# A contiguous write and a strided read in an exponential, with a new set of planner priorities

## Chip, cores and metric

The kernel runs on one core of a Trainium2 chip. The metric is the device time in microseconds of one execution. Before the change the median of three runs is 550.88 us (548.93 to 553.61).

## What is computed

Three stages follow each other; each takes the output of the one before. Attention is of the Nyström kind with 32 landmarks, on 4 batches, 8 heads, 576 tokens, 64 features. MoE sends each token to one of 8 experts (capacity 576) and applies two layers. MoE2 is one dense pair of layers with a PReLU between.

```python
q_lm = q.reshape(B, H, m, S // m, D).mean(axis=3)
k_lm = k.reshape(B, H, m, S // m, D).mean(axis=3)
A, Bm, C = sm(q, k_lm), sm(q_lm, k_lm), sm(q_lm, k)      # softmax of scaled scores
Z = Bm.transpose(0, 1, 3, 2) / (norm1(Bm) * norminf(Bm) + 1e-06)
for _ in range(6):
    Z = 2 * Z - Z @ Bm @ Z
attn = A @ Z @ C @ v
...
logits = x @ w_gate                                      # x: 2304 x 512
expert_idx = np.argmax(logits, axis=1)
h = np.maximum(np.einsum('ecd,edf->ecf', disp, w1), 0.0)  # 512 -> 1024
y = np.einsum('ecf,efd->ecd', h, w2)                      # 1024 -> 512
out[i] = gate_w[i] * y[expert_idx[i], pos[i]]
...
h = x @ w_in                                              # 512 -> 2048
g = np.maximum(h, 0.0) + alpha * np.minimum(h, 0.0)
return g @ w_out                                          # 2048 -> 512
```

## The kernel before

**Work.** Attention goes by (batch b, group g of four heads), eight pairs. MoE and MoE2 then go by entry: an entry is one pair of a batch and an expert that has tokens there. With these inputs there are three. The first entry is done ahead of a loop, in one stretch with attention; the loop at L1796 does the other two. Products are made from two or three products of 16-bit halves, so weights are scaled by a power of two and split into a high and a low half (`split`, for WI and WO; MW for an expert's first layer, W for its second). The scale of a weight comes from a sum of squares (`squares`), which one small matmul adds up over partitions (`scale_of`: the matmul that reads ss_w1, ss_w2, ss_wi or ss_wo), and a few narrow VectorE operations behind it (tot, sc, s, r).

An entry has four stages on TensorE: the first MoE layer (`moe_h`: mm<-xT,MW), the second (`moe_y`: mm<-W,hgA), the first MoE2 layer (`moe2_h`: mm<-yA,WIa and mm<-yB,WIa, 256 and 320 tokens wide, later WIb), and the second (`moe2_out`: mm<-WO,hgA, then hgB). An expert's first layer uses only 32 landmark rows: 16 matmuls turn W1 into them (`landmark_rows`), and MW is their scaled, split form. The tiles hgA and hgB hold MoE2's hidden values. The weights of the next entry are loaded and converted while an entry runs (`next_w1_late`, `next_w2`); W1 is loaded over tiles that the raw WO occupied. The stores of zeros to the output (`clear`, out<-zero) stand in SP's queue, as all plain loads.

**Order.** Each engine takes its instructions strictly in its queue's order. That order is not written by hand. Operations are yielded by generators, the streams, and `Plan.run` (L346) issues them one at a time from a model of durations. It takes the operation with the earliest modelled start; another stream with a better (lower) rank that uses the same engine goes first if it starts before `by()`. The rank of a stream is a constant in the source, and many are set anew on the way.

```python
def by(self, s, x):
    return s.start + min(s.op.ns, self.patience + self.EAGER * (s.rank - x.rank))
```

`.takes(us)` sets the modelled duration of an operation. `keep_warm` (L248) puts filler matmuls (L1728, mm<-zero,ones or big<-zero,ones, 128x256) into a fresh PSUM tile where the model lets TensorE wait. The loop body is planned anew by the same function with few streams of fixed ranks.

**The exponential of C.** `attend_c` (L672) makes the scores of 32 landmarks against 576 tokens for four heads in a PSUM tile `big` of two banks, takes the maximum (mx) and its scaled negative (nm), and ScalarE writes the exponential to EC in SBUF with its row sum. Four transposes on TensorE read EC, the copy to CT follows, and then the product with v.

Of the kernel before, what the change touches and what calls it, by code (L numbers as in the profile page):

```python
# [18 lines left out]
LM = 32  # L19
TG = 18  # L20
# [4 lines left out]
RANKS = [[-19.821, -51.876], [-35.858, 62.800], [-39.803, -18.825], [-37.270, -58.893]]  # L25
# [179 lines left out]
class Plan:  # L205
# [5 lines left out]
    EAGER = -30.723  # L211
# [173 lines left out]
class Kernel:  # L385
# [41 lines left out]
    def constants(self):  # L427
# [29 lines left out]
        self.streams["constants"].own = -31.506  # L457
# [72 lines left out]
    def loads(self):  # L530

        for b in range(self.B):
            for g in range(2):
                heads = slice(4 * g, 4 * g + 4)
                self.streams["loads"].own = RANKS[b][g] + -31.591
                for nm, src in (("k", self.k), ("q", self.q)):
                    self.raw[nm, b, g] = t = yield Get(self.S["qk"])
                    yield self.dq.dma_start(t, src[b, heads].rearrange("h (p j) d -> (h p) j d", j=TG))
                    self.have.add((nm, b, g))
                if (b, g) == (0, 0):  # L540
                    self.streams["values"] = yield Fork(self.values(), 47.215)

    def values(self):

        for b in range(self.B):
            for g in range(2):
                heads = slice(4 * g, 4 * g + 4)
                if (b, g) != (0, 0):
                    self.streams["values"].own = RANKS[b][g] + -39.752
                self.raw["v", b, g] = t = yield Get(self.S["v"])  # L550
                src = self.v[b, heads]
                yield self.dq.dma_start(t[:, :, :4].rearrange("p h t d -> p h (t d)"), src[:, : 4 * P].rearrange("h (p t) d -> p h (t d)", t=4))
                yield self.dq.dma_start(t[:64, :, 4], src[:, 4 * P :].rearrange("h p d -> p h d"))
                self.have.add(("v", b, g))
                if (b, g) == (0, 0):
                    self.tc.prologue_barrier()

    def sums(self):


        gp = self.gp
        for b in range(self.B):
            for g in range(2):
                self.streams["sums"].own = RANKS[b][g] + -31.456
# [24 lines left out]
    def turn(self):  # L589
# [8 lines left out]
        for b in range(self.B):  # L598
            for g in range(2):
                self.streams["turn"].own = RANKS[b][g] + -19.707  # L600
# [71 lines left out]
    def attend_c(self, b, g):  # L672
# [18 lines left out]
        apart = EC.rearrange("p (m j w) -> p w j m", m=LM, w=2)  # L691
        yield act.activation(apart, tokens.rearrange("p (w j m) -> p w j m", w=2, m=LM), AF.Exp, bias=nm2[:, 0:1], scale=0.125 / TG, accum_out=sums[:, 0:1])
# [41 lines left out]
    def attend_a(self, b, g):  # L734
# [32 lines left out]
        self.streams["store", b, g] = yield Fork(self.store(b, g, parts), 46.670)  # L767
# [8 lines left out]
    def attention_post(self, bs):  # L776
# [79 lines left out]
        if b == 0:  # L856
            self.streams["post0"].own = -44.230
# [53 lines left out]
        for n, bb in enumerate(bs):  # L911
# [18 lines left out]
            if bb == 0:  # L930
                yield from self.first_expert(L[0:1, 0, 0, :])
                self.streams["post0"].own = -38.923
            yield Fork(self.used(bb, AT))
        self.have.add(("x", bs[-1]))
        if b:
            yield self.until(("routed", 0))
            self.streams["post"].own = 12.961
# [37 lines left out]
    def route(self, bs, L):  # L975
# [82 lines left out]
        if b == 0:  # L1058
# [5 lines left out]
            self.streams["post0"].own = 46.684  # L1064
# [138 lines left out]
    def landmark_rows(self, MT, slots, late=0.0):  # L1203
# [26 lines left out]
        scale = yield Fork(self.scale_of("w1", 4), -39.828)  # L1230
# [38 lines left out]
    def early(self):  # L1269
# [12 lines left out]
        self.streams["early_loads"] = yield Fork(loads(), -32.383)  # L1282
# [42 lines left out]
    def convert(self, name, n, amax=None, low="d", load=None, first=0):  # L1325
# [9 lines left out]
        scale = yield Fork(self.scale_of(name, n // 2, amax), -31.812)  # L1335
# [12 lines left out]
    def weight2(self, name, src, amax, low, first=0):  # L1348
# [9 lines left out]
        if name == "wi":  # L1358
            self.streams["wi_loads"] = yield Fork(self.fetch(name, src, range(first, 16, 2), arrived), -58.911)
        else:  # L1360
            self.streams["wo_loads"] = yield Fork(self.fetch(name, src, range(first, 16, 2), arrived), -31.034)
# [246 lines left out]
    def pre(self):  # L1608

        yield self.until(("P", 0, 0), ("P", 0, 1), *([("used", self.n_early - 4)] if self.n_early else ["early"]))  # L1610
        self.streams["first"].own = -38.041
# [4 lines left out]
        self.streams["first"].own = 13.553  # L1616
# [3 lines left out]
        self.streams["first"].own = -20.015  # L1620
# [3 lines left out]
    def weights(self):  # L1624
# [4 lines left out]
        self.streams["rows"] = yield Fork(self.landmark_rows(self.MT[:, 0:2], [self.big] * 2), -30.753)  # L1629
        yield self.until("early")  # L1630
        self.streams["weights"].own = -32.417
        yield from self.load_expert(bass.ds(e0, 1), ["w2"])
        self.streams["weights"].own = 1.715
# [85 lines left out]
    def run(self):  # L1719
# [15 lines left out]
        with tc.manual_schedule(engines={ET.PE, ET.DVE, ET.Activation, ET.Pool, ET.SP}):  # L1735
# [24 lines left out]
            for _ in range(10):  # L1760
# [5 lines left out]
                "constants": Stream(self.constants(), 1.014),  # L1766
                "post0": Stream(self.attention_post([0]), -36.880),
                "first": Stream(self.pre(), -20.351),
                "weights": Stream(self.weights(), -20.511),
                "rooms": Stream(self.rooms(), -33.672),  # L1770
                "post": Stream(self.attention_post(list(range(1, self.B))), -36.946),
                "early": Stream(self.early(), 61.182),
                "wi": Stream(self.weight_in(), -30.891),
                "wo": Stream(self.weight_out(), 52.666),
                "clear": Stream(self.clear(), 17.278),
                "experts": Stream(self.experts(), -66.764),
                "out": Stream(self.first_out(), -40.666),
                "next": Stream(self.first_next(), -44.222),
                "next_w1": Stream(self.next_w1_late(), -44.548),
                "next_w2": Stream(self.next_w2('d'), -68.688),  # L1780
            }
            for b in range(self.B):
                for g in range(2):
                    self.streams["c", b, g] = Stream(self.attend_c(b, g), RANKS[b][g] + -50.062)
                    self.streams["a", b, g] = Stream(self.attend_a(b, g), RANKS[b][g] + 12.563)
# [41 lines left out]
```

## Time and profile before

| | us |
|---|---|
| median of three runs | 550.88 |
| profiled execution | 550.0 |
| its span from first to last instruction | 548.1 |
| TensorE busy | 517.7 (94%) |
| VectorE busy | 297.8 (54%) |
| ScalarE busy | 261.0 (48%) |
| GpSimd busy | 93.6 (17%) |
| mean granted clock of TensorE | 0.992 |

The busy shares are means over stages with different limits, and TensorE's contains the fillers. So the page's shares are read first, then the same shares by stage, and in the stages the timeline: a row of it holds the start, the duration, and in brackets the engine's idle time just before together with what ended it. A row with a count is a run of like instructions; its duration reaches from the first start to the last end, and a matmul's end lies past the start of the next.

### The profile page before, as it was taken

Reading aid. Unit: us, or ns where it says so; the run is one execution under the profiler, and the core shown is the slowest. Engines: PE = TensorE matmul, PEld = TensorE weight load, DVE = VectorE, ACT = ScalarE, POOL = GpSimd, SP = SyncE. Lnnn points to the kernel's source line nnn. Section 1 sums busy time; section 2 is a strip of 40 time slices with the busy share of each in tenths; the row PEclk is TensorE's granted clock in tenths of the full one; section 3 lists DMA queues with packets and bytes.
Section 4 is the critical chain, followed back from the end, with each engine's and each line's share of the span. In section 5 each row is a group of like instructions: output and inputs, shape, how many; then the busy total and the mean of one; then the engine's idle time right before and its main releaser. Section 6 shows DMA issues by size and latency. Waiting matters only on the chain. (4 is left out here: it accounts for less than half of the span.)

```text
span 548.1 us, 12276 instructions
## 1 busy us (share of the span) xinstructions
PE 517.7 (94%) x4888; PEld 341.5 (62%) x4888; DVE 297.8 (54%) x712; ACT 261.0 (48%) x579; POOL 93.6 (17%) x139
## 2 busy tenths in 40 slices
PE   9899999999867899799889999999999999999996
PEld 6777777776355676344465586864467567675444
DVE  6987898898996795500062365870005246585000
ACT  4767648753764598401152256850004235783000
POOL 3899611010231122101100000000110000000101
PEclk9999999999999999999989999999999999999999
DMA  8898657517599555001002266000100227300100
GB/s 334 304 323 281 202 171 252 178 59 272 165 230 263 167 156 197 0 1 39 28 22 20 48 155 221 1 1 19 39 20 12 37 47 225 135 1 1 38 20 30
DMA packets 50692, 64.64 MB, mean 118 GB/s; under 512 B 20320, under 2 KB 34032, under 8 KB 50640
## 3 DMA queue, kind: packets, MB, share of 16 engines
q1 hardware_dynamic: 49536, 60.34, 36.0%
q0 software_dynamic: 1104, 3.54, 1.7%
q8 instruction: 40, 0.66, 0.5%
q14 instruction: 12, 0.10, 0.0%
HBM read 49.50 MB, written 10.62 MB: 110 GB/s over the span
## 5 line engine op out<-in xcount | busy, mean ns | idle before, releaser
L81 PEld LDWEIGHTS <-hgA 128*128 128x128 f16 (+1 forms) x864 | 70.7, 102 | 69.8 <-issue 5.8
L81 PEld LDWEIGHTS <-WIa 128*128 128x128 f16 x864 | 84.6, 99 | 33.1 <-issue 10.7
L81 PE MATMUL mm<-WO,hgA 128*128 128x512 f16 (+1 forms) x432 | 73.0, 344 | 0.0
L81 PE MATMUL mm<-WO,hgB 128*128 128x512 f16 (+1 forms) x432 | 72.8, 344 | 0.0
L81 PE MATMUL mm<-W,hgA 128*128 128x512 f16 (+1 forms) x432 | 72.2, 344 | 0.1
L81 ACT ACTIVATE st<-mm,fac 128x512 f32<-128x512 f32 (+1 forms) x15 | 9.7, 644 | 125.2 <-PE mm L81 123.1
L81 PE MATMUL mm<-yB,WIa 128*128 128x320 f16 x432 | 63.1, 304 | 4.2 <-DVE x_lst L81 2.7
L81 POOL DMA_INDIRECT out<-st,idxc x12 | 11.9, 990 | 292.2 <-ACT st L81 289.7
L81 PEld LDWEIGHTS <-hgB 128*128 128x128 f16 (+1 forms) x432 | 35.4, 102 | 35.5 <-issue 2.5
L81 PE MATMUL mm<-yA,WIa 128*128 128x256 f16 x432 | 50.8, 273 | 3.5 <-DVE xh L81 1.7
L81 ACT ACTIVATE g<-mm 128x256 f32<-128x256 f32 (+1 forms) x96 | 38.9, 413 | 16.8 <-PE mm L81 10.9
L81 DVE SCALAR_TENSOR_TENSOR mm<-g,oma,mm 128x256 f32<-128x256 f32 (+1 forms) x80 | 40.9, 517 | 10.3 <-ACT g L81 9.6
L81 PE MATMUL mm<-xT,MW 128*128 128x320 f16 (+1 forms) x288 | 38.6, 294 | 4.6 <-ACT MW L81 3.3
L81 PEld LDWEIGHTS <-MW 128*128 128x128 f16 x288 | 28.5, 101 | 13.1 <-ACT MW L81 3.4
L1728 PE MATMUL mm<-zero,ones 128*128 128x256 f16 x201 | 29.0, 286 | 6.5 <-DVE hgB L81 3.1
L1728 PEld LDWEIGHTS <-ones 128*128 128x128 f16 x253 | 24.1, 102 | 16.4 <-issue 10.6
L81 PEld LDWEIGHTS <-WIb 128*128 128x128 f16 x288 | 28.2, 99 | 8.7 <-issue 1.8
L81 ACT ACTIVATE junk<-mm 128x512 bf16<-128x512 f32 (+1 forms) x27 | 15.4, 569 | 30.3 <-PE mm L81 30.2
L81 ACT COPY qkT<-mm 128x512 f32<-128x512 f32 (+1 forms) x48 | 22.5, 523 | 14.8 <-PE mm L81 14.7
L81 ACT ACTIVATE hgA<-mm 128x256 f16<-128x256 f32 (+1 forms) x48 | 19.5, 409 | 17.1 <-PE mm L81 16.6
L81 DVE SCALAR_TENSOR_TENSOR hgA<-mm,hgA 128x256 f16<-128x256 f32 (+1 forms) x48 | 21.5, 454 | 11.3 <-ACT hgA L81 11.0
L81 ACT CAST hgA<-mm 128x256 f16<-128x256 f32 (+1 forms) x40 | 15.9, 397 | 23.6 <-DVE mm L81 23.6
(286 smaller groups left out, 748.8 us busy)
## 6 DMA issues: line engine op xcount, KB each, us to landing
W<-in_moe_w SPq DMA_DIRECT2D x8, 1024.0 KB, 8.9
st<-in_moe_w_out SPq DMA_DIRECT2D x16, 512.0 KB, 4.6
hgA<-in_moe_w_in SPq DMA_DIRECT2D x10, 512.0 KB, 7.1
qk<-in_k SPq DMA_DIRECT2D x8, 576.0 KB, 5.5
qk<-in_q SPq DMA_DIRECT2D x8, 576.0 KB, 6.7
out<-zero SPq DMA_DIRECT2D x18, 256.0 KB, 6.2
v<-in_v SPq DMA_DIRECT2D x8, 512.0 KB, 4.9
W<-in_moe_w SPq DMA_DIRECT2D x8, 512.0 KB, 5.7
```

What stands on the lines that cost most here:

```text
L81: r = getattr(self.lane.engine, name)(*a, **k)
L1728: nc.tensor.matmul(o[:, :256], self.ones16, self.zero.bitcast(F16), start=True, stop=True)
```

## The change

In `attend_c` the loop order of the exponential is turned. Before, ScalarE read the 576 scores in the order in which they lie (w, j, m) and wrote each to its place in EC, 18 elements from the last one. After, it writes EC in order (m, j, w), and reads PSUM at a stride: neighbours in the order of work lie 288 elements apart, in the two banks. The plan is told 1.0 us for it.

All other lines of the diff are numbers: RANKS, EAGER and the ranks of the streams. Three places of some forty are shown.

```diff
-RANKS = [[-19.821, -51.876], [-35.858, 62.800], [-39.803, -18.825], [-37.270, -58.893]]
+RANKS = [[-74.375, -56.288], [-49.431, -65.912], [71.374, -74.373], [72.660, -62.802]]
...
-    EAGER = -30.723
+    EAGER = -62.784
...
-        apart = EC.rearrange("p (m j w) -> p w j m", m=LM, w=2)
-        yield act.activation(apart, tokens.rearrange("p (w j m) -> p w j m", w=2, m=LM), AF.Exp, bias=nm2[:, 0:1], scale=0.125 / TG, accum_out=sums[:, 0:1])
+        turned = tokens.rearrange("p (w j m) -> p m j w", w=2, m=LM)
+        yield act.activation(EC.rearrange("p (m j w) -> p m j w", m=LM, w=2), turned, AF.Exp, bias=nm2[:, 0:1], scale=0.125 / TG, accum_out=sums[:, 0:1]).takes(1.0)
...
-        scale = yield Fork(self.scale_of(name, n // 2, amax), -31.812)
+        scale = yield Fork(self.scale_of(name, n // 2, amax), -63.884)
```

The numbers move instructions everywhere ahead of the loop. The orders of the engines in the loop stay. TensorE's queue has 253 fillers before and 173 after: 189 and 152 ahead of the first matmul on xT, 48 and 19 from there to the first on yA, 16 and 2 behind it.

TensorE, end of the first entry and start of the loop, before (ss_w is the sum of squares of the next W1; its matmul stands last, and the loop follows):

```order
L81 LDWEIGHTS hgB
L81 MATMUL mm_3673<-WO,hgB 64x256
L81 MATMUL mm_3524<-ss_w_113,ones 128x4
L1792 TENSOR_LOAD x_lst
L1796 COMPARE_AND_BRANCH
L1796 UNCONDITIONAL_BRANCH
L1822 BRANCH_PREFETCH_HINT
L81 LDWEIGHTS MW
L81 MATMUL mm_3888<-xT,MW 128x256
```

The same matmul after the change, mm_3510, with that of W2 ahead of it, between the first three token tiles of `moe2_out` and the last two:

```order
L81 LDWEIGHTS hgB
L81 MATMUL mm_3334<-WO,hgB 128x512
L81 MATMUL mm_3563<-ss_w_114,ones 128x4
L81 MATMUL mm_3510<-ss_w_113,ones 128x4
L81 LDWEIGHTS hgA
L81 MATMUL mm_3575<-WO,hgA 128x512
```

It moved ahead of 144 matmuls on WO; the loop's first matmul now stands directly behind the last of them.

TensorE, the sum of squares of WO. Before, it stands between two groups on yB and WIa in the middle of `moe2_h`:

```order
L81 LDWEIGHTS WIa
L81 MATMUL mm_3054<-yB,WIa 128x320
L81 MATMUL mm_3057<-ss_wo,ones 128x8
L81 LDWEIGHTS WIa
L81 MATMUL mm_3078<-yB,WIa 128x320
```

After, it stands between groups on WIb:

```order
L81 LDWEIGHTS WIb
L81 MATMUL mm_3233<-yA,WIb 128x256
L81 MATMUL mm_3239<-ss_wo,ones 128x8
L81 LDWEIGHTS WIb
L81 MATMUL mm_3255<-yB,WIb 128x320
```

It moved from a place with 17 groups of 12 matmuls behind it to one with three, and the matmuls on WO follow those.

VectorE, the splits of WO, before: behind s_wo they alternate with the evictions of `moe2_h` (mm<-g, g<-g and hgB<-mm).

```order
L81 SCALAR_TENSOR_TENSOR g_19_3161<-g_19_3161,oma,mm_3138 128x256
L81 SCALAR_TENSOR_TENSOR WO<-W_86,s_wo,WO 128x2x512
L81 SCALAR_TENSOR_TENSOR g_20_3179<-g_20_3179,oma,mm_3154 128x320
L81 SCALAR_TENSOR_TENSOR WO<-W_87,s_wo,WO 128x2x512
L81 SCALAR_TENSOR_TENSOR mm_3177<-g_21_3231,oma,mm_3177 128x256
L81 SCALAR_TENSOR_TENSOR WO<-MW,s_wo,WO 128x2x512
L81 TENSOR_TENSOR hgB<-mm_3177,hgB 128x256
L81 SCALAR_TENSOR_TENSOR mm_3197<-g_22_3249,oma,mm_3197 128x320
L81 SCALAR_TENSOR_TENSOR g_23_3251<-g_23_3251,oma,mm_3212 128x256
L81 SCALAR_TENSOR_TENSOR WO<-MW,s_wo,WO 128x2x512
```

After: the last evictions of `moe2_h` and the splits stand together, and the operations on the next entry's weights (tot_w and what follows) behind all eight splits.

```order
L81 TENSOR_TENSOR hgB<-mm_3233,hgB 128x256
L81 SCALAR_TENSOR_TENSOR WO<-W_86,s_wo,WO 128x2x512
L81 TENSOR_TENSOR iw_101<-r_wi,r_wo 128x1
L81 SCALAR_TENSOR_TENSOR mm_3255<-g_30_3282,oma,mm_3255 128x320
L81 TENSOR_TENSOR fac<-fac,iw_101 128x5
L81 SCALAR_TENSOR_TENSOR g_31_3303<-g_31_3303,oma,mm_3274 128x256
L81 SCALAR_TENSOR_TENSOR WO<-W_86,s_wo,WO 128x2x512
L81 TENSOR_TENSOR hgB<-mm_3255,hgB 128x320
L81 SCALAR_TENSOR_TENSOR g_32_3322<-g_32_3322,oma,mm_3302 128x320
L81 SCALAR_TENSOR_TENSOR WO<-W_86,s_wo,WO 128x2x512 x2
L81 SCALAR_TENSOR_TENSOR WO<-W_87,s_wo,WO 128x2x512
L81 SCALAR_TENSOR_TENSOR WO<-MW,s_wo,WO 128x2x512 x2
```

The splits moved to the end of the stage, and the conversions of the next W2 from between the last evictions to behind the splits.

In `moe_y` the first six matmuls on hgA stand, after the change, directly behind the small products that make Gm (wgs,MT), and the first product on Gm behind those six; before, 22 fillers and 12 products on Gm lay between. 12 of the stage's 19 fillers are left ahead of wgs,MT.

## Rows read from the trace of the kernel before

**Rows 1.** Busy time by stage: window, length, each engine (instructions), granted clock, DMA share, GB/s.

```profile
0.00:96.00 96.00, 91.94 (x1465) 71.06 (x1466) 80.38 (x205) 63.39 (x148) 52.90 (x104) 1.00 0.80 267
96.00:155.00 59.00, 56.40 (x791) 38.67 (x790) 53.98 (x115) 36.12 (x68) 7.71 (x4) 1.00 0.52 165
155.00:219.00 64.00, 53.48 (x436) 39.83 (x437) 49.47 (x113) 43.50 (x95) 15.98 (x15) 0.97 0.72 209
219.00:275.50 56.50, 50.13 (x301) 23.98 (x300) 9.38 (x17) 12.53 (x23) 6.34 (x6) 1.00 0.05 19
275.50:548.10 272.60, 265.77 (x1900) 167.93 (x1900) 104.58 (x266) 105.42 (x248) 10.69 (x11) 0.99 0.20 54
```

**Rows 2.** Timeline of TensorE, 96.5 to 123.2: start, duration, engine, line, operation, tiles, shapes, count.

```profile
97.42 0.87 PE L81 MATMUL mm<-RW 32*32 32x64 f32 x48
...
100.71 0.75 PE L81 MATMUL big<-qkT 64*32 64x256 f32 x32
...
118.37 2.58 PE L1728 MATMUL mm<-zero,ones 128*128 128x256 f16 x22
```

**Rows 3.** TensorE, 155 to 189.5; in brackets the idle time before and its releaser.

```profile
158.08 1.47 PE L81 MATMUL mm<-yA,WIa 128*128 128x256 f16 x12 [1.68 <-DVE xh L81]
...
177.68 9.82 PE L81 MATMUL mm<-yB,WIa 128*128 128x320 f16 x60 [2.71 <-DVE x_lst L81]
```

**Rows 4.** Timeline of VectorE around 176.

```profile
176.78 0.69 DVE L81 TENSOR_SCALAR MW<-st 128x1024 int32<-128x1024 int32 x1 [3.87 <-DMA st<-in_moe_w_out]
```

**Rows 5.** TensorE at the start of the second layer, 216 to 230.

```profile
219.23 1.46 PE L81 MATMUL mm<-WO,hgA 128*128 128x512 f16 x6
223.78 1.03 PE L1728 MATMUL mm<-zero,ones 128*128 128x256 f16 x8 [3.10 <-DVE hgB L81]
```

**Rows 6.** VectorE in the same place.

```profile
219.53 1.29 DVE L81 SCALAR_TENSOR_TENSOR W<-W,s_w 128x1024 f16<-128x1024 f32 x1 [1.15 <-ACT W L81]
```

**Rows 7.** TensorE at the end of the first entry and the start of the loop.

```profile
254.44 8.76 PE L81 MATMUL mm<-WO,hgA 128*128 128x512 f16 x72
...
271.84 0.39 PE L81 MATMUL mm<-ss_w,ones 128*128 128x4 f32 x2
275.50 13.60 PE L81 MATMUL mm<-xT,MW 128*128 128x256 f16 x96 [3.27 <-ACT MW L81]
```

**Rows 8.** TensorE between the two passes of the loop.

```profile
410.85 11.92 PE L81 MATMUL mm<-xT,MW 128*128 128x256 f16 x96 [1.25 <-ACT st L81]
```

**Rows 9.** Busy time and granted clock of two short windows.

```profile
177.60:183.00 5.40, 5.32 (x29) 3.34 (x29) 4.44 (x8) 3.09 (x8) 1.18 (x2) 0.70 0.89 265
...
275.50:279.00 3.50, 3.50 (x21) 2.65 (x22) 1.96 (x5) 0.99 (x3) 0.97 (x1) 0.62 0.13 44
```

**Rows 10.** ScalarE groups by shape: count, busy us, mean ns, idle before.

```profile
L81 ACT ACTIVATE EC<-big,nm 128x576 f32<-128x576 f32 x8 | 10.8, 1347 | 5.2 <-DVE nm L81 5.2
...
L81 ACT ACTIVATE T<-T 128x576 f32<-128x576 f32 x8 | 5.4, 689 | 1.9 <-DVE T L81 1.9
```

**Rows 11.** VectorE groups by shape, two reductions.

```profile
L81 DVE TENSOR_REDUCE WIa<-qk 128x64 f32<-128x1152 f32 x3 | 6.5, 2169 | 3.4 <-DMA qk<-in_k 3.4
...
L81 DVE TENSOR_REDUCE mx<-big 128x1 f32<-128x576 f32 x8 | 6.0, 750 | 2.6 <-PE big L81 1.8 <-PE mm L81 0.6
```

**Rows 12.** Timeline of VectorE behind the copy of L.

```profile
67.57 2.18 DVE L81 SCALAR_TENSOR_TENSOR WIa<-hgA,WIa 128x1024 int32<-128x1024 int32 x1
...
73.17 0.13 DVE L81 TENSOR_SCALAR e0i<-m 1x1 int32<-1x1 f32 x1
```

**Rows 13.** VectorE at ss_wo and the splits of WO.

```profile
191.24 0.16 DVE L81 TENSOR_REDUCE tot_wo<-mm 128x1 f32<-128x8 f32 x1
...
193.59 1.28 DVE L81 SCALAR_TENSOR_TENSOR WO<-W,s_wo,WO 128x1024 f16<-128x1024 f32 x1 [0.56 <-ACT WO L81]
...
207.72 1.27 DVE L81 SCALAR_TENSOR_TENSOR WO<-xT,s_wo,WO 128x1024 f16<-128x1024 f32 x1
```

**Rows 14.** The page, part 6, one DMA issue: count, KB each, us to landing.

```profile
W<-in_moe_w SPq DMA_DIRECT2D x8, 1024.0 KB, 8.9
```

More of the change, by code (lines that the diff above doesn't have):

```diff
@@ L456, in constants @@
         self.have.add("constants")
-        self.streams["constants"].own = -31.506
+        self.streams["constants"].own = -64.376
         def iota(name, n, pattern, base=0, mult=0, parts=P, dt=F32):
@@ L534, in loads @@
                 heads = slice(4 * g, 4 * g + 4)
-                self.streams["loads"].own = RANKS[b][g] + -31.591
+                self.streams["loads"].own = RANKS[b][g] + -54.682
                 for nm, src in (("k", self.k), ("q", self.q)):
@@ L563, in sums @@
             for g in range(2):
-                self.streams["sums"].own = RANKS[b][g] + -31.456
+                self.streams["sums"].own = RANKS[b][g] + -55.120
                 i = 2 * b + g
@@ L856, in attention_post @@
         if b == 0:
-            self.streams["post0"].own = -44.230
+            self.streams["post0"].own = -64.244
         big = yield Get(self.big)
@@ L936, in attention_post @@
             yield self.until(("routed", 0))
-            self.streams["post"].own = 12.961
+            self.streams["post"].own = -67.282
         yield from self.route(bs, L)
@@ L1229, in landmark_rows @@
         yield ended(kids)
-        scale = yield Fork(self.scale_of("w1", 4), -39.828)
+        scale = yield Fork(self.scale_of("w1", 4), -61.376)
         yield ended([scale])
@@ L1280, in loads @@
                 self.have.add(("loaded", i))
-        self.streams["early_loads"] = yield Fork(loads(), -32.383)
+        self.streams["early_loads"] = yield Fork(loads(), 65.505)
         kids = []
@@ L1610, in pre @@
         yield self.until(("P", 0, 0), ("P", 0, 1), *([("used", self.n_early - 4)] if self.n_early else ["early"]))
-        self.streams["first"].own = -38.041
+        self.streams["first"].own = -64.283
         yield from self.moe_h(True)
@@ L1615, in pre @@
         yield self.dve.tensor_copy(self.idxc, self.idx0)
-        self.streams["first"].own = 13.553
+        self.streams["first"].own = -52.364
         yield from self.moe_y((0, 1, 2, 3, 4), self.gate[:, 0], True)
@@ L1619, in pre @@
         yield self.until("rooms")
-        self.streams["first"].own = -20.015
+        self.streams["first"].own = -61.768
         yield from self.moe2_h(True)
@@ L1628, in weights @@
         yield from self.load_expert(bass.ds(e0, 1), ["w1"])
-        self.streams["rows"] = yield Fork(self.landmark_rows(self.MT[:, 0:2], [self.big] * 2), -30.753)
+        self.streams["rows"] = yield Fork(self.landmark_rows(self.MT[:, 0:2], [self.big] * 2), -64.966)
         yield self.until("early")
-        self.streams["weights"].own = -32.417
+        self.streams["weights"].own = -54.431
         yield from self.load_expert(bass.ds(e0, 1), ["w2"])
-        self.streams["weights"].own = 1.715
+        self.streams["weights"].own = 64.801
         yield from self.convert("w2", 8, low='d')
@@ L1765, in run @@
                 "sums": Stream(self.sums(), 2),
[L1766 to L1780, printed above, removed]
+                "constants": Stream(self.constants(), 56.007),
+                "post0": Stream(self.attention_post([0]), -64.166),
+                "first": Stream(self.pre(), -58.952),
+                "weights": Stream(self.weights(), -54.630),
+                "rooms": Stream(self.rooms(), -55.921),
+                "post": Stream(self.attention_post(list(range(1, self.B))), -55.955),
+                "early": Stream(self.early(), 70.830),
+                "wi": Stream(self.weight_in(), 70.305),
+                "wo": Stream(self.weight_out(), 72.429),
+                "clear": Stream(self.clear(), 73.613),
+                "experts": Stream(self.experts(), 70.932),
+                "out": Stream(self.first_out(), -64.384),
+                "next": Stream(self.first_next(), -69.294),
+                "next_w1": Stream(self.next_w1_late(), -69.303),
+                "next_w2": Stream(self.next_w2('d'), -60.504),
             }
```

20 lines of the change are left out of this document (10 added, 10 removed).

## The prediction, made before the changed kernel ran

> **What bounds the kernel now.** I read the table by stage first [rows 1]. In each stage TensorE is the busiest engine, with VectorE near it only up to 219, so what is to be won must come out of TensorE's queue: idle time, matmuls that compute nothing, or time at the lower clock. The stages show where that is. From 275.5 on, in the two passes of the loop, TensorE is busy 265.77 of 272.60 us. The diff leaves the engines' order in the loop as it is, so this stays a block of 272.6 us. Before the loop, idle TensorE lies mostly in 155 to 219 (64.00 − 53.48 = 10.5 us, the first layer of MoE2) and 219 to 275.5 (6.4 us). Up to 155 TensorE looks full, but part of it is fillers: TensorE's queue holds 253 of them. Twenty-two in a row last 2.58 us [rows 2], so each takes at most 0.12 us of the queue, about 0.11 once the last one's end is taken off; 253 × 0.11 = 28 us hold nothing but warmth.
>
> Then TensorE's timeline at the long waits. In MoE2's first layer they go from 1.68 us at 158.08 to 2.71 at 177.68, and VectorE ends each of the two [rows 3]. The one at 177.68 shows a chain: just before it VectorE itself stood 3.87 us for a transfer of w_out [rows 4], and only then read x_lst, which freed the PSUM tile that TensorE wanted. At the second layer's start TensorE does six matmuls, stands 3.10 us, and does eight fillers [rows 5]; hgB comes late because VectorE converts the next expert's weights ahead of it, 1.29 us a piece [rows 6]. At the loop's start TensorE waits 3.27 us for MW [rows 7]; the same place between the two passes costs 1.25 us [rows 8].
>
> [...]
>
> **The change, part by part.** *The exponential of C.* Eight instructions of 128x576 take 1347 ns each. T's exponential, the same 576 elements without a stride, takes 689 ns [rows 10]; the write at a stride costs about 0.65 us. The new form writes contiguously but reads PSUM at a stride, and no ScalarE row here reads so. Lower bound: that read is free, 8 × 0.65 = 5.2 us less of ScalarE. The nearest row of a read at a stride is VectorE's reduction of k, 1152 elements in 2169 ns, 1.88 ns each, against 750/576 = 1.30 in a contiguous one [rows 11], a factor of 1.45; 1.45 × 0.69 = 1.0 us, still 0.35 us less. The engines differ, so 1.35 us, no gain at all, stays as the outer bound; I take 0.7 to 1.0.
>
> [...]
>
> What is the exponential worth on the path? In 0 to 96 ScalarE is busy 63.39 us and TensorE 91.94 [rows 1]. A shorter exponential gets sooner out of the way of copies that feed a TensorE which is nearly full, fillers among it. I take 0 by itself, between −5.2 and, if reads collide, +1.
>
> *Fillers.* The queue holds 173 instead of 253: 80 × 0.11 = 8.8 us less. That is a gain only where the work behind them is ready sooner. Ahead of the first MoE matmul there are 189 before and 152 after, from there to MoE2 48 and 19, later 16 and 2. Ahead of the MoE most stand in a chain whose steps stay (the first expert's index, loading W1, landmarks, scale); fewer fillers don't shorten a chain. Behind the copy of the routing logits L, VectorE does a conversion of WIa of 2.18 us and two shorter ones before it computes the index e0i at 73.17, 5.6 us later [rows 12]; in the new order five operations on T stand there instead, 5 × 0.75 = 3.8 us at the rate of a reduction of 576 elements [rows 11], and the waits between them. I take 1 us of this. **Term 1: −1** (−4 to 0).
>
> *The MoE stage, 96 to 155.* Here 29 fillers go, 3.2 us, and one iteration product and one set of scores (0.87 + 0.75 = 1.6 us [rows 2]) move ahead, into time where fillers stood. The run of 22 at 118.37 covered the wait for Gm; in the new queue the second layer's first six matmuls stand there. TensorE's idle time in the stage is 59.00 − 56.40 = 2.6 us. Low end −3.2 − 1.6 − 2.6 = −7.4, high end 0 (each missing filler turns into idle time). **Term 2: −3.**
>
> *MoE2's first layer.* WI's scale is taken 42 matmuls into the second MoE layer instead of 12, so its conversions come later, and VectorE is no less tight than now (49.47 of 64 us [rows 1]). x_lst goes behind the first groups on B, away from the place where it cost 2.71 us and then (1 − 0.70) × 5.4 = 1.6 us of clock, 4.3 together. Against it, w_out's later loads come behind nine stores of zeros in SP's queue. **Term 3: −2**, half of the 4.3; ends −4.3 and +4 (one more wait of that kind).
>
> *The second layer's start.* ss_wo's product moves to within three groups of the layer's end, WO's splits come right behind it, and the next expert's conversions only behind those. So the 3.10 us and the eight fillers, 8 × 0.11, lose their cause: 4.0 us. In their place WO's first split must be there in time. From ss_wo's total on VectorE to the end of the first split takes 193.59 + 1.28 − 191.24 = 3.6 us [rows 13]; three groups of 12 matmuls, at 0.12 (yA, 1.47/12 [rows 3]) to 0.15 us each, are about 4.8 us. A split comes every 2.0 us ((207.72 − 193.59)/7), and TensorE uses one for 18 matmuls of 0.24 (1.46/6 [rows 5]), 4.3 us; so only the first can be late. The next expert's W1 can load only when the splits have freed W. Its landmarks stand 72 matmuls (17 us) into the layer; a load of 1024 KB lands in 8.9 us [rows 14]. **Term 4: −3**; ends −4 and +4.
>
> *The loop's start.* ss_w1's product was TensorE's last before the loop; now it stands ahead of the last 144 matmuls, which take 271.84 − 254.44 = 17.4 us [rows 7], against 5 us of VectorE work on MW. From that product to the loop's first matmul it is 275.50 − 271.84 = 3.66 us; it becomes the ordinary 1.25, so −2.4. The 96 matmuls behind it take 13.60 us with the clock down and 11.92 in the other pass [rows 7, 8], so −1.7. **Term 5: −4**; ends −4.1 and −3. It is the one that I hold safest.
>
> Sum: −1 − 3 − 2 − 3 − 4 = −13. The profiled execution took 550.0 us (its span and 1.9 around it); 550.0 − 13 = 537.0. The median of the runs shown, 550.88, is 0.9 above that execution: 537.9, said as 538.
>
> **Rivals.** *Fillers give way to idle time.* Terms 1 to 3 come to nothing, 4 and 5 stay: 550.9 − 7 = 543.9; with WO or W1 late by 2, 546. For it: fillers stand where the plan expects a wait. Against: at Gm there is other work to put in their place.
>
> *Nothing comes of it.* Where a wait is no longer filled, the clock can fall: 1.6 us behind one wait of 2.71 us. Four such places take 6.4 us, which with the rival above leaves 550.
>
> *Slower: WO uncovered.* Eight splits take 16 us on VectorE (193.59 to 209.0 [rows 13]); before, matmuls covered all of it; now 4.8 us do. If the evictions of hgB stand behind the splits in VectorE's queue, and TensorE waits for PSUM behind each, 11 us lie open and W1 lands late by as much. In place of term 4, with the other terms at half, that is 550.9 − 5 + 11 = 557. It decides from about 10 us of uncovered splits on. Against it: TensorE uses up splits more slowly (4.3 us) than they come (2.0).
>
> **How the numbers follow.** Forecast 0.57, fillers to idle time 0.20, nothing 0.14, slower 0.09. A measurement of this kernel can tell about 1% from no change, so faster is below 545.4 and slower above 556.4. Faster: 0.57 + 0.16 of the first rival = 0.73. Slower: 0.05 of the last rival. Same: the rest, 0.22. The forecast's own range is 532 to 543: with all of term 2 it would be 533.5, with something from the exponential 532. The whole range goes up to 549, into "nothing"; it leaves out the slower rival, half of "nothing" and a low tail of 0.03, together 0.19.
>
> **What would show it.** EC's exponential at 0.7 to 1.0 us; the first matmul on yA at about 151 instead of 155; behind the first six WO matmuls no wait above 1 us; the loop's first matmul at about 262.5, some 1.3 us behind the last WO matmul, and a clock of 1.00 in the 96 matmuls behind it. Wrong would be: several us of waiting at WO or at the next W1's landmarks (term 4), idle time at Gm as long as the fillers were (term 2), over 10.5 us idle in MoE2's first layer (term 3).

## The result, and the profile after

The changed kernel takes 532.84 us (median of four executions, 531.43 to 534.53) against 550.22 for the kernel before, run beside it (548.93 to 553.61). The ratio is 0.968, with an interval of 0.962 to 0.973: 17.4 us faster. The forecast was 538, within 532 to 549. The profiled execution took 532.0 us, its span 527.9, at a mean granted clock of 0.998.

The same table by stage as [rows 1]: window, length, busy time and instructions of TensorE, weight loads, VectorE, ScalarE and GpSimd, granted clock, DMA share, GB/s. The windows end where the same stages end.

```profile
0.00:97.90 97.90, 89.92 (x1508) 69.22 (x1509) 81.32 (x201) 58.23 (x142) 47.84 (x104) 1.00 0.75 247
97.90:149.70 51.80, 51.21 (x681) 34.88 (x680) 46.20 (x122) 33.31 (x65) 3.44 (x2) 1.00 0.57 185
149.70:205.50 55.80, 49.03 (x400) 38.25 (x399) 48.47 (x99) 38.31 (x86) 18.94 (x16) 1.00 0.67 183
205.50:257.00 51.50, 50.89 (x326) 23.70 (x324) 18.75 (x29) 24.80 (x39) 6.66 (x6) 1.00 0.33 109
257.00:527.90 270.90, 264.09 (x1900) 167.07 (x1899) 102.91 (x264) 105.44 (x248) 11.28 (x12) 1.00 0.19 55
```

| stage | before, us | after, us | difference | term of the sum |
|---|---|---|---|---|
| to the first matmul on xT | 96.0 | 97.9 | +1.9 | 1: −1 |
| MoE, to the first on yA | 59.0 | 51.8 | −7.2 | 2: −3 |
| MoE2's first layer, to the first on WO | 64.0 | 55.8 | −8.2 | 3: −2 |
| second layer, to the loop's first matmul | 56.5 | 51.5 | −5.0 | 4 and part of 5 |
| the loop | 272.6 | 270.9 | −1.7 | rest of 5 |
| span | 548.1 | 527.9 | −20.2 | −13 |
| time outside the span | 1.9 | 4.1 | +2.2 | not in the sum |

The landmarks of the next W1 (1.95 us of TensorE) moved from the third stage to the fourth. So the first layer really gave 8.2 − 1.9 = 6.3 by these windows, and the second layer with the loop 5.0 + 1.9 + 1.7 = 8.6.

TensorE's timeline at the places of the steps:

```profile
116.64 1.47 PE L1728 MATMUL mm<-zero,ones 128*128 128x256 f16 x12
118.05 0.58 PE L81 MATMUL mm<-wgs,MT 64*32 64x8 f32 x48
118.56 1.47 PE L81 MATMUL mm<-W,hgA 128*128 128x512 f16 x6
119.86 2.19 PE L81 MATMUL mm<-Gm,AT 128*128 128x8 f32 x24
...
182.80 1.79 PE L81 MATMUL mm<-yB,WIa 128*128 128x320 f16 x12 [3.70 <-DVE g L81]
...
205.50 15.70 PE L81 MATMUL mm<-WO,hgA 128*128 128x512 f16 x72
221.13 1.95 PE L81 MATMUL mm<-W,mtn 64*32 64x512 f32 x32
...
238.56 0.50 PE L81 MATMUL mm<-ss_w,ones 128*128 128x4 f32 x4
...
257.01 11.92 PE L81 MATMUL mm<-xT,MW 128*128 128x256 f16 x96 [0.62 <-ACT st L81]
```

Where 22 fillers stood between the products wgs,MT and those on Gm [rows 2], six matmuls on hgA stand now and no filler; the 12 fillers ahead of wgs,MT were there before the change too. The second layer starts at 205.50 with 72 matmuls in one piece, where the kernel before stood 3.10 us after six [rows 5]. The loop's first matmul waits 0.62 us instead of 3.27, and its 96 matmuls take 11.92 us instead of 13.60 [rows 7]. Behind the first matmul on xT one long wait is left, 3.70 us at 182.80. VectorE in the same place, and the first split of WO:

```profile
179.88 0.69 DVE L81 TENSOR_SCALAR MW<-st 128x1024 int32<-128x1024 int32 x1 [3.59 <-DMA st<-in_moe_w_out]
...
203.44 1.28 DVE L81 SCALAR_TENSOR_TENSOR WO<-W,s_wo,WO 128x1024 f16<-128x1024 f32 x1 [0.63 <-ACT WO L81]
```

The wait of [rows 4] is still there, 3.59 us against 3.87, for the same transfer of w_out; only what TensorE then lacks is g and no longer x_lst. SP's queue shows why the transfer is late:

```profile
162.05 1.38 SPq L81 DMA_DIRECT2D st<-in_moe_w_out  x2
163.47 8.42 SPq L81 DMA_DIRECT2D out<-zero  x9
171.99 1.62 SPq L81 DMA_DIRECT2D st<-in_moe_w_out  x2
```

Nine stores of zeros take 8.42 us of the queue ahead of it. The exponential of C, by shape, with T's beside it [rows 10]:

```profile
L81 ACT ACTIVATE EC<-big,nm 128x576 f32<-128x576 f32 x8 | 6.0, 748 | 5.7 <-DVE mx L81 3.8 <-DVE nm L81 1.9
...
L81 ACT ACTIVATE T<-T 128x576 f32<-128x576 f32 x8 | 5.5, 691 | 1.3 <-DVE T L81 1.3
```

EC, with its strided read of PSUM, takes 57 ns more than T, which reads and writes its own tile in order. So the edit saves 0.60 us an instruction, nearly the 0.65 of the lower bound.

### The profile page after: what moved, and what is told of

Read it like the earlier page. It is cut to its first block, busy times and chain, and to the rows that moved or that the text cites. A ratio compares the mean times of both kernels' runs of the same rounds, so it can differ in the third digit from the quotient of the medians.

```text
span 527.9 us, 12141 instructions
## 1 busy us (share of the span) xinstructions
PE 505.1 (96%) x4808; PEld 333.1 (63%) x4808; DVE 297.6 (56%) x712; ACT 260.1 (49%) x579; POOL 88.2 (17%) x139
## 4 chain that ended last, share of the span: by engine, by line
PE 74%; DVE 10%; issue 6%; DMA 3%; POOL 2%; ACT 1%; POOLq 0%; SPq 0%; ACTq 0%; DVEq 0%
PE mm L81 70%; PE big L81 2%; DMA out<-st,idxc 2%; PE mm L1728 2%; DVE MW L81 1%; DMA st<-in_moe_w_out 1%; DVE W L81 1%; DVE WIa L81 1%; DVE mm L81 1%; DVE T L81 1%; DVE hgA L81 1%; POOL WIa L81 1%; DVE g L81 1%; POOL hgB L81 1%; DVE mx L81 0%
## 5 line engine op out<-in xcount | busy, mean ns | idle before, releaser
L81 PE MATMUL mm<-yB,WIa 128*128 128x320 f16 x432 | 61.5, 299 | 4.9 <-DVE g L81 3.7
L81 PE MATMUL mm<-xT,MW 128*128 128x320 f16 (+1 forms) x288 | 36.9, 286 | 2.4 <-ACT st L81 1.8
L81 DVE TENSOR_TENSOR hgA<-mm,hgA 128x256 f16<-128x256 f32 (+1 forms) x40 | 18.2, 455 | 14.1 <-ACT hgA L81 13.9
L81 ACT ACTIVATE junk<-W 128x1024 bf16<-128x1024 f32 x21 | 22.2, 1056 | 7.5 <-DMA W<-in_moe_w 7.0
```

Of the source, the lines that this page charges most:

```text
L81: r = getattr(self.lane.engine, name)(*a, **k)
```

## The experiments

Times are given as ratios to the kernel before, run beside each kernel, since its own median moved between 550.2 and 555.2; in parentheses stands the 95% interval.

**Which part of the change.** `exp_only` is the kernel before with the turned exponential alone; `old_exp_new_ranks` is the changed kernel with the old exponential (planned at 1.0 us, so that the order stays).

```diff
--- before
+++ exp_only
-        apart = EC.rearrange("p (m j w) -> p w j m", m=LM, w=2)
+        turned = tokens.rearrange("p (w j m) -> p m j w", w=2, m=LM)
...
--- after
+++ old_exp_new_ranks
-        turned = tokens.rearrange("p (w j m) -> p m j w", w=2, m=LM)
+        apart = EC.rearrange("p (m j w) -> p w j m", m=LM, w=2)
```

> The kernel before with only the exponential of C turned; every queue has the same order as before. Theory (the exponential itself is off the path, the order makes the gain): EC takes 0.75 us as in the changed kernel instead of 1.35, and the time is 549 to 550.5, at most 1 us under before. Rival (the exponential is the gain): 8 x 0.6 = 4.8 us or more less, 545 or lower.

> The changed kernel with the exponential of before (read in order, write at a stride), still planned at 1.0 us, so that every queue keeps the changed kernel's order. Theory: EC takes 1.35 us again and the time rises by 0 to 2 us over the changed kernel's 532.8, to 533 to 535, since the order was planned for a shorter one. Rival (the exponential is the gain): 537.5 or more.

Measured: 1.0005 (0.997 to 1.004) and 0.963 (0.958 to 0.968). ScalarE's group in the second:

```profile
L81 ACT ACTIVATE EC<-big,nm 128x576 f32<-128x576 f32 x8 | 10.8, 1346 | 5.1 <-DVE mx L81 3.8 <-DVE nm L81 1.4
```

In `exp_only` EC takes 748 ns and nothing is gained. With the old exponential of 1346 ns the new order is as fast as the change. So the gain is the order; the exponential alone is worth nothing that the interval of some 2 us to either side would show.

**The second layer and the loop's start (terms 4 and 5).** `before_wo_late` holds WO's scale and splits back until the end of the first layer is near (three groups of 12 matmuls stand behind the sum of squares). `before_w1_early` changes one rank, so that the next W1's sum of squares stands ahead of most WO matmuls. `after_w1_late` puts that sum behind the last of them in the changed kernel.

```diff
--- before
+++ before_wo_late
+        if name == "wo":
+            yield self.until("h14")
...
+            if first and x[:2] == (14, 256):
+                self.have.add("h14")
...
--- before
+++ before_w1_early
-        scale = yield Fork(self.scale_of("w1", 4), -39.828)
+        scale = yield Fork(self.scale_of("w1", 4), -39.828 if not late else -45.0)
...
--- after
+++ after_w1_late
+        if late:
+            yield self.until("out done")
...
+        self.have.add("out done")
```

> The kernel before, old exponential, old ranks, with one condition more: WO's scale and splits wait until the product for f = 14 on B is issued, so they stand at the end of MoE2's first layer as in the changed kernel; the next W1's landmarks and both sums of squares move behind the first WO matmuls by themselves. Up to MoE2 nothing moves. Theory (VectorE co-limits MoE2's first layer, TensorE alone the second; ten us of splits change from the first to the second): besides the 4 us at the loop's start and the 4 us at WO, MoE2's first layer gets 2 to 4 us shorter than its 64.3 beyond the 1.9 us of landmarks that leave it; 550 - 4 - 2 - 3 = 541, 538 to 543. Rival (only the named waits go, VectorE's load does not matter): 543 to 545, and the first layer at 62 us. Rival (splits uncovered): a wait of several us at WO.

> The kernel before, old exponential, with one rank changed: the scale of the next W1 goes ahead of the second layer's matmuls. Only the product of ss_w1 and what hangs on it (MW's split) move, ahead of most of the WO matmuls. Theory (term 5): the wait of 3.27 us at the loop's start becomes about 1.25 or less, the first 96 matmuls take 11.9 us instead of 13.6, together 3.5 to 4.5 us less: 546 to 547. Rival (something else makes the loop begin sooner): within 1 us of before.

> The changed kernel with the sum of squares of the next W1 put back behind the last WO matmul, ahead of the loop (that of W2 goes with it). Theory (term 5): the wait at the loop's start is 3 us or more again and the clock falls behind it, 3.5 to 4.5 us more from the first instruction to the last. The time outside that span is 4.1 us in the changed kernel and 1.8 in the kernel before; in before_w1_early and before_wo_late, where that sum of squares stands ahead, it is 4.6 to 4.8. If it depends on this place, it falls back to about 1.8 and the time rises only by 1 to 2 us, to 534 to 535; if it depends on something else, it stays at 4.1 and the time rises to 536 to 537.

Measured: 0.986 (0.981 to 0.991), 1.003 (1.000 to 1.006), 0.979 (0.974 to 0.984). TensorE in `before_wo_late`:

```profile
178.66 9.80 PE L81 MATMUL mm<-yB,WIa 128*128 128x320 f16 x60 [3.21 <-DVE x_lst L81]
...
216.83 15.70 PE L81 MATMUL mm<-WO,hgA 128*128 128x512 f16 x72
...
268.34 11.92 PE L81 MATMUL mm<-xT,MW 128*128 128x256 f16 x96 [0.62 <-ACT st L81]
```

TensorE runs 72 WO matmuls without a stop, and as the plan also moves both sums of squares ahead of the last 144 matmuls, the loop starts after 0.62 us. From the first matmul on WO to the loop's it is 268.34 − 216.83 = 51.5 us, as in the changed kernel. The first layer (first yA at 155.39) takes 61.4, 1.95 of the saving being the landmarks; its wait for x_lst stays. So terms 4 and 5 are reproduced on the old order, and taking the splits out of the first layer gives it only 1 us: the 2 to 4 us that I expected of a freer VectorE did not come, and the 544.4 us measured are the rival's. What frees the 72 matmuls is not the splits' place but that of W2's conversions: in `before_late_clear` below the splits stay ahead among the evictions, only the conversions go behind the last hgB (the first starts at 217.91, behind hgB at 216.85; in the kernel before at 219.53, ahead of hgB at 223.25), and the 72 run in one piece there too.

`before_w1_early` missed its −4. TensorE at its loop start:

```profile
275.45 5.40 PE L81 MATMUL mm<-xT,MW 128*128 128x256 f16 x48 [0.70 <-ACT st L81]
...
281.66 6.68 PE L81 MATMUL mm<-xT,MW 128*128 128x320 f16 x48 [0.80 <-DVE hgA L81]
```

The wait fell from 3.27 to 0.70 as meant, and 2.0 us came back between the first matmul on xT and the loop; a new wait of 0.80 us stands among the first 96 matmuls, and the loop to the end is 273.5 against 272.6. Two other things eat what is left: in this profiled execution the first matmul on xT came 1.9 us later, ahead of anything that the edit moves, and the time outside the span is 4.4 to 4.7 us where the kernel before has mostly 1.7 to 2.1. `after_w1_late` overshot its +4: by the ratios it is (0.979 − 0.968) × 550 = 6 us slower than the change, and its span is 10 us longer, of which 9.0 lie between the first matmul on WO and the loop. Its time outside the span fell to 2.1 to 2.3 us in three executions (3.2 in one).

```profile
255.43 0.61 PE L81 MATMUL mm<-ss_w,ones 128*128 128x4 f32 x4
...
265.50 13.66 PE L81 MATMUL mm<-xT,MW 128*128 128x256 f16 x96 [9.46 <-ACT W L81]
```

W2's sum went late along with W1's, its conversions stood among those of MW on ScalarE, the last of them ended at 265.45, and the wait grew to 9.46 us. It shows how dear this place can be, and again 13.66 us for the 96 matmuls behind a long wait; it is no clean price for W1's sum alone.

**Fillers and the MoE stage (terms 1 and 2).** `before_nofill_moe` leaves out the 48 fillers between the first matmul on xT and the first on yA; `wo_late_nofill_moe` does that on `before_wo_late`. `before_first_ahead` gives the first entry's stream another rank (−38.041 for 13.553) through `moe_y`. `after_nofill_all` issues only the first 19 of the changed kernel's 173 fillers. Fillers compute nothing; no work is left out.

```diff
--- before
+++ before_nofill_moe
+            made[0] += 1
+            if 189 < made[0] <= 237:
+                return
...
--- before
+++ before_first_ahead
-        self.streams["first"].own = 13.553
+        self.streams["first"].own = -38.041
...
--- after
+++ after_nofill_all
+            made[0] += 1
+            if 19 < made[0] <= 173:
+                return
```

> The kernel before without its 48 fillers between the first matmul on xT and the first on yA; they are planned but not issued, so every other instruction keeps its place. Theory (a filler that is issued where the work behind it is ready, or will be soon, delays it): the stretch from the first xT to the first yA, 58.9 us, loses 2 to 4 us and the time falls to 546 to 549. Rival (fillers stand only where TensorE would wait anyway): the stretch stays at 58.9 within 0.7 us, the idle time grows by 4 to 5 us, and the time stays within 1 us; if the granted clock falls behind the longer waits, it gets up to 3 us longer.

> The kernel with WO's scale and splits late (544.4 us), now also without the 48 fillers of the MoE stage. If the effects add, it gives what the fillers alone give on top: 540.5 to 542.5 by the theory that fillers delay work, 544 to 545 by the rival that they only fill waits. Either way it stays above the changed kernel's 532.8, because the attention work and the conversions of WI are where they were.

> The kernel before, old exponential, with one rank changed: the main stream keeps its good rank of the first MoE layer (-38.0 in place of 13.6) through the second. The plan moves what follows from that: the second layer's matmuls stand ahead of the products on Gm, and VectorE does the results of the second layer (pyc to xh) ahead of the conversions of WI and WO, as in the changed kernel. Theory (the gain in the MoE stage and the shorter waits at the start of MoE2's first layer come from ready main work standing ahead of side work, not from the missing fillers): the stretch from the first xT to the first yA, 58.9 us, loses 4 to 7 us, the waits for xh (1.68 and 2.65 us with eight fillers) shrink, and the time falls by 4 to 9 us, to 542 to 547. Rival (the gain needs the attention work that the changed kernel moves ahead of the MoE): the stretch stays within 2 us, 549 to 551; or the side work comes late and is waited for instead, 551 or more.

> The changed kernel without its fillers except the first 19 at the program's start: 154 are planned but not issued, all else keeps its place. Theory (what is left of the fillers keeps the clock up in waits that exist anyway): the granted clock in attention falls from 1.00 to 0.7 to 0.95, and the time rises by 1 to 6 us, to 534 to 539. Rival (fillers delay work here too): the time falls by 1 to 5 us, to 528 to 532, and the clock stays above 0.97.

Measured: 1.011 (1.007 to 1.015); 0.992 (0.988 to 0.996), against 0.986 (0.981 to 0.991) with them, and at 548.1 us above both ranges expected; 0.988 (0.984 to 0.993); 0.961 (0.956 to 0.966). Windows of `before_nofill_moe` in the stage, columns as above:

```profile
96.70:124.99 28.29, 24.46 (x541) 19.32 (x539) 25.38 (x52) 17.25 (x37) 2.81 (x2) 0.94 0.39 125
...
124.99:156.00 31.01, 29.98 (x204) 17.31 (x202) 28.53 (x62) 18.71 (x31) 4.89 (x2) 0.95 0.61 197
```

and its TensorE at the first matmuls on hgA:

```profile
124.99 2.74 PE L81 MATMUL mm<-W,hgA 128*128 128x512 f16 x6
```

The stage takes 59.4 us without fillers and 58.9 with. Of the 5.3 us of fillers (48 × 0.11) 2.3 became idle time, and the clock fell (six matmuls of 1.47 us take 2.74). In `wo_late_nofill_moe`, whose queues are the same up to MoE2, the clock fell further and the stage took 64.9 us against 58.5 in `before_wo_late`:

```profile
98.60:163.50 64.90, 61.28 (x743) 41.23 (x740) 55.31 (x122) 36.98 (x68) 7.68 (x4) 0.82 0.48 155
```

So leaving the fillers out did not make the MoE stage shorter in either. The 1.011, some 6 us and twice what I allowed for a falling clock, is not the price of this stage alone: 0.5 of the 4.9 us by which the span grew lie in it, and most of the rest in the second layer and the loop's start, which the edit leaves as they were but whose clock was 0.94 and 0.80 instead of 1.00 and 0.87 (the loop's first 96 matmuls take 14.83 us instead of 13.60). In `before_first_ahead` it became shorter because work was put there:

```profile
115.18 23.62 PE L81 MATMUL mm<-W,hgA 128*128 128x512 f16 x144
...
149.94 2.19 PE L81 MATMUL mm<-Gm,AT 128*128 128x8 f32 x24
...
176.88 4.04 PE L81 MATMUL mm<-yA,WIa 128*128 128x256 f16 x24 [4.16 <-DVE g L81]
```

The matmuls on hgA run in one piece and the stage loses 2.6 us, but the products on Gm, done later, cost the first layer as much: from the first xT to the first WO it is 123.9 us against 123.2. Its time fell within the 542 to 547 us expected, but not for the reason expected: its gain came at WO and the loop, where its plan, too, put W2's conversions behind the first WO matmuls (256.81) and W1's sum ahead of the last 144. The time outside its span is 1.8 to 2.1 us.

In the new order, fewer fillers do shorten something. VectorE's copy of L in the changed kernel and in `after_nofill_all`, and TensorE in the first layer of the latter:

```profile
69.06 0.20 DVE L81 COPY L<-mm 128x40 f32<-128x40 f32 x1 [0.48 <-PE mm L81]
...
64.89 0.20 DVE L81 COPY L<-mm 128x40 f32<-128x40 f32 x1
```

```profile
177.94 3.36 PE L81 MATMUL mm<-yB,WIa 128*128 128x320 f16 x12 [3.82 <-DVE g L81]
```

Between these two profiled executions L comes 4.2 us sooner, and the first matmul on yA at 144.7 instead of 149.7. One execution is a poor measure of this part, so here are all with the new order: the index e0i behind L is computed at 71.9 to 74.0 us in the four kernels with fillers there, and at 68.8 and 70.6 in the two without (the other is `after_clear_nofill` below); from it to the first matmul on yA it is 76 us in all six. So the fillers held the routing chain up, by 1.3 to 5.2 us. They also kept the clock up: without them it is 0.94 in the 90 us to the first matmul on xT (1.00 with them, over 97.9 us), where the theory expected it, and the time fell all the same, as the rival said. Half of the 5 us is lost in MoE2's first layer, part of it where 12 matmuls behind the wait take 3.36 us instead of 1.79; the first on WO comes 2.5 us earlier (202.97). In time, 0.961 and the change's 0.968 have overlapping intervals.

**MoE2's first layer (term 3).** `after_late_clear` and `before_late_clear` hold all 18 stores of zeros back until the last load of w_out is issued. In the changed kernel only SP's queue changes by it; on the kernel before, the next W2's conversions also move, behind the last hgB.

```diff
-        yield self.until('y')
+        yield self.until('y', ("got", "wo", 14))
```

> The changed kernel with one condition more: the stores of zeros wait until the last load of w_out is issued. Only SP's queue changes: all 18 stores stand behind the loads. Theory (VectorE's wait of 3.59 us for w_out at 179.88, and with it TensorE's 3.70 at 182.80, comes from the nine stores ahead of that load in SP's queue): both waits shrink below 1.5 us and the time falls by 2 to 4 us, to 529 to 531. Rival (the load waits for its buffer or for bandwidth, not for its place in the queue): same waits, same time within 1 us. Second rival: the zeros then collide with the load of the next W1 or delay the first rows of the output, and the time rises by 1 to 3 us.

> The kernel before, old exponential and old ranks, with the stores of zeros behind the last load of w_out in SP's queue; the other queues change by a few rows only. Theory (a load of w_out that stands behind stores of zeros is what VectorE waits for at 176.78 and 184.95, 3.87 and 2.85 us, and TensorE behind it at 177.68 and 188.95): these waits shrink below 1.5 us each, the clock stays up behind 177, and the stretch from the first yA to the first WO matmul, 64.3 us, gets 3 to 5 us shorter: 545 to 548. Rival (in this order VectorE would be late there anyway): TensorE's waits only move to the next place, within 1 us of before.

Measured: 0.957 (0.953 to 0.962), that is 1.1% below the change, and 0.979 (0.971 to 0.988). SP, VectorE and TensorE in `after_late_clear`:

```profile
157.74 23.79 SPq L81 DMA_DIRECT2D st<-in_moe_w_out  x8
181.56 16.87 SPq L81 DMA_DIRECT2D out<-zero  x18
```

```profile
174.35 0.67 DVE L81 TENSOR_SCALAR MW<-st 128x1024 int32<-128x1024 int32 x1
```

```profile
177.81 1.79 PE L81 MATMUL mm<-yB,WIa 128*128 128x320 f16 x12 [0.59 <-DVE g L81]
```

VectorE no longer waits for the transfer, and TensorE's 3.70 us become 0.59. Its first matmuls on xT and yA:

```profile
96.04 2.13 PE L81 MATMUL mm<-xT,MW 128*128 128x256 f16 x18
...
147.82 1.48 PE L81 MATMUL mm<-yA,WIa 128*128 128x256 f16 x12
```

The first matmul on WO comes at 200.63, so the first layer takes 52.8 us instead of 55.8. These 3.0 us are what the edit shows; the other 1.9 of the 4.9 us by which the span is shorter lie ahead of the first matmul on xT, where the queues are those of the changed kernel and executions differ by as much. In the kernel before, SP's queue has the zeros ahead of the load of [rows 4] as well:

```profile
160.82 3.56 SPq L81 DMA_DIRECT2D out<-zero  x5
...
166.38 1.45 SPq L81 DMA_DIRECT2D out<-zero  x2
...
170.58 1.00 SPq L81 DMA_DIRECT2D st<-in_moe_w_out  x2
```

In `before_late_clear`:

```profile
175.46 10.77 PE L81 MATMUL mm<-yB,WIa 128*128 128x320 f16 x78
...
215.78 15.70 PE L81 MATMUL mm<-WO,hgA 128*128 128x512 f16 x72 [0.59 <-DVE tot_w L81]
...
267.92 13.60 PE L81 MATMUL mm<-xT,MW 128*128 128x256 f16 x96 [3.27 <-ACT MW L81]
```

```profile
174.00:180.00 6.00, 6.00 (x49) 4.37 (x48) 6.00 (x14) 4.36 (x11) 1.82 (x2) 1.00 0.99 311
```

The wait for x_lst [rows 3] is gone and the clock stays at 1.00 where it was 0.70 [rows 9]. The first layer takes 58.6 us instead of 64.3: 2.71 for that wait, 1.45 for one on hgA further on, and 1.6 of clock make 5.8. The zeros stood in front of the loads, and that was the cause in both orders. (The second layer is 4.1 us shorter here too, because of the moved W2 conversions; that is why the time fell further than the 545 to 548 us expected. The loop's wait of 3.27 stays.)

**Both edits together.** `after_clear_nofill` is the changed kernel with the late zeros and without all but 19 fillers.

> Both edits that made the changed kernel faster, together: the zeros stand behind the last load of w_out in SP's queue, and no filler is issued but the first 19. If they add: 532.8 - 4.7 - 2.8 = 525.3, and less by 1 to 2 us more, since without the fillers the wait of 3.8 us for w_out let the clock fall, and that wait is gone: 523 to 525.5. Rival (each only brings the same wait forward): 527 to 528.

Measured: 526.31 us, 0.952 (0.948 to 0.956), the lowest ratio of all, between the theory's range and the rival's. The two edits gave 1.1% and 0.7% alone, and 1.6% together. It is clear of the change (0.962 to 0.973), but its interval overlaps that of the late zeros alone (0.953 to 0.962), so what the missing fillers add to them is not shown by the time.

## Why the prediction was right or wrong

**The exponential** was priced right at its lower bound (748 ns, 0.6 us less), and right in being worth nothing on the path: `exp_only` at 1.0005, and the order alone at the full gain. I had taken 0.7 to 1.0 us, the 1.0 from VectorE's strided reduction of k [rows 11], and left 1.35, no gain at all, as the outer bound. The factor of 1.45 from that reduction did not carry over to this read by ScalarE: 748 ns, strided read and all, beside 691 for T, and 1347 for the strided write [rows 10].

**Term 1 (−1; +1.9 in this profile).** The first matmul on xT stands between 96.0 and 98.6 in the profiled executions of the eight kernels with this part in the old order, and between 96.0 and 97.9 in the four with it in the new order and all its fillers, so the term is about 0. L to e0i did become shorter, 4.9 us in all four against 5.7 to 7.2 in the eight. But from e0i to the first matmul on xT it is 23.9 to 24.6 us in the new order and mostly 22.8 in the old: what I took from the first part was lost in the second. And the step "fewer fillers don't shorten a chain" failed: without them e0i came 1.3 to 5.2 us sooner.

**Term 2 (−3; −7.2).** The mechanism was right, the size was the low end of its range, −7.4: TensorE's busy time fell by 5.2 us (29 fillers, 3.2, and the moved attention, 1.6) and its idle time from 2.6 to 0.6. I had held half back for missing fillers that turn into idle time. `before_nofill_moe` shows what comes of only leaving them out: no shorter stage, idle time and a lower clock. What paid was ready work in their place. `before_first_ahead` reached −2.6 with another order of the same work and gave it back later, so no single move tried here carries the 7 us alone.

**Term 3 (−2; −6.3).** Worked out in part only, and the largest miss: 6.3 lies outside the term's own ends, −4.3 and +4. Idle time fell from 10.5 to 6.8 us, 14 fillers (1.5 us) went, and the clock stayed at 1.00. The wait that I meant to lose came back as I wrote in "against it": 3.70 us behind nine zeros. But the clock did not fall after it, where in the kernel before it stood at 0.70 over 5.40 us [rows 9], the 1.6 us of clock in the term:

```profile
182.80:188.30 5.50, 5.50 (x45) 4.36 (x45) 5.18 (x9) 3.82 (x10) 0.79 (x1) 1.00 0.30 94
```

And two waits that I had not priced are gone: those for xh, which VectorE evicted behind weight conversions. One is in [rows 3], 1.68; the other, in the kernel before:

```profile
162.32 1.03 PE L1728 MATMUL mm<-zero,ones 128*128 128x256 f16 x8 [2.65 <-DVE xh L81]
```

I stopped at the longest wait of the stage, and left the sum of the others (10.5 us of idle time) out of the term. That the xh waits went by the order on VectorE is read from the traces. The nearest run is `before_first_ahead`: there VectorE has done xh by 142.8, ten us ahead of the first matmul on yA, and no wait for xh is left, but waits of 2.30 us for hgA and 4.16 for g stand in the layer instead. What the xh waits alone are worth in the new order no run isolated.

**Term 4 (−3; −3.6).** Right, by its steps. From the first WO matmul to the end of the stage's last it is 52.6 us before and 50.9 after, the landmarks' 1.95 included. The first split ended at 204.72, 0.8 us ahead of its use: the slower rival, WO uncovered, did not occur.

**Term 5 (−4; −4.7).** Right: 3.66 us became 0.62, and 13.60 became 11.92. `before_wo_late` gives the same two numbers on the old order.

**Outside the span (0; +2.2).** The sum held these 1.9 us fixed; they became 4.1. So the error of 5 us is 7 too little within the span and 2 too little lost outside. That the time lies in the range at all, 0.8 us above its lower end, is luck in part: without the 2.2 us lost outside the span, which nothing in the prediction foresaw, it would have fallen below. The rivals "fillers give way to idle time" and "nothing" did not occur: from the first matmul on xT to the loop TensorE's idle time fell by 2.0, 3.7 and 5.8 us in the three stages.

## What to carry to other kernels

Work that is ready, put where TensorE would wait, shortened the MoE stage by 7.2 us; leaving fillers out of the same stage did not shorten it, and the clock fell to 0.94 and 0.82. In front of a short dependent chain fillers cost time here: e0i came 1.3 to 5.2 us sooner without them, at a lower clock. Read all waits of a stage, not the longest alone, and follow each to the queue that is late: stores that nobody waits for, ahead of a load in one queue, cost 5.7 us of a stage before the change and 3.0 after. Compare stage by stage: a part that no edit touched moved by 2 us from execution to execution. A faster instruction on an engine that is not the last to finish was worth nothing by itself here.

## What the runs showed that was not expected

The time outside the span takes two values. It is mostly 1.7 to 2.1 us in the kernel before, `exp_only`, `before_nofill_moe`, `before_first_ahead` and `before_late_clear`, and 4.0 to 4.9 in nearly all executions of the changed kernel, `old_exp_new_ranks`, `before_w1_early`, `before_wo_late` and the others. It follows the order and not the work. No view shows what fills it. The guess that it hangs on the early place of W1's sum is borne out by `after_w1_late`, where that sum is late and the time fell to 2.1 to 2.3 us in three of four executions, but it falls with `before_first_ahead`, which has the early place and 1.8 to 2.1 us. It stays open, and is worth about 2.3 us.

Two waits of nearly the same length, 3.70 us in the changed kernel and 3.82 without its fillers, were followed by a granted clock of 1.00 (the row shown for term 3) and of 0.56. The window of the changed kernel without its fillers:

```profile
177.90:184.00 6.10, 6.06 (x28) 3.81 (x28) 4.69 (x8) 3.28 (x9) 0.79 (x1) 0.56 0.38 114
```

TensorE's work ahead of them was alike: 11.60 of 12.40 us busy at 165.0 to 177.4 in the changed kernel, 11.70 of 12.50 at 160.0 to 172.5 without its fillers, the clock 1.00 in both. So the length of a wait alone did not tell what the clock does behind it. What else decided is not settled by these runs.
